# The first round's tile list made in two parts behind the last softmax, and the last batch's gate, choice and ranks woven with the first dense tiles

## The chip, the cores and the metric

The kernel runs on one core of one Trainium2 chip. Its time is the device time of one execution in microseconds (us), and the number that counts is the median over runs. Inside a core five engines work beside one another, each through its own list of instructions in order: PE (TensorE, matrix products; its weight loads are shown apart as PEld), DVE (VectorE), ACT (ScalarE), POOL (GpSimd) and SP (SyncE, which here only issues DMAs and reads values into registers). An instruction waits for others through semaphores. DMAs issued by POOL and by SP go to two different queues that share sixteen DMA engines.

## The reference: what is computed

Attention over chunks, and then a mixture of experts on its result.

```python
for c in range(nc):                       # 24 chunks of 32 queries
    q_c = q[:, :, c*32:(c+1)*32]
    k_full = concat(mem_k, k[:, :, left:right])   # 8 memory keys + up to 56 keys around the chunk
    a = softmax(q_c @ k_full.T / 8)
    out[:, :, c*32:(c+1)*32] = a @ v_full
x = out as (3072 tokens, 512)             # 4 batches of 768 tokens, 8 heads of 64
y_dense = relu(x @ w1_dense) @ w2_dense
logits = x @ w_gate                       # 8 experts
expert = argmax(logits); gate_w = softmax(logits)[expert]
y_moe[t] = gate_w[t] * (relu(x[t] @ w1[expert[t]]) @ w2[expert[t]])
return y_dense + y_moe
```

All matrices of the experts are 512 by 512.

## The kernel before

Sixteen attention steps come first, one for each pair of heads of each of the four batches (`for i in range(NPAIR)`, step 15 is the last). A step computes its own values and, ahead of time, the scores and the softmax of the next step. Its parts: `scores` (PE), `maximum` and `softmax` (DVE, then an exponential on ACT), `copy_v(i, 0)` on POOL and `copy_v(i, 1)` on DVE (line 333, they copy rows of the values that two chunks share, and wait for those rows' DMA), `probs_back` (PE transposes, ACT copy), `values` (PE, line 418), `scaled` (DVE, lines 429 and 430, giving x of the pair), `gate_part` (six PE transposes of x, line 450, copied by ACT, line 453), `gate_sum` (PE, line 475, three products with the gate's weights) and `gate_add` (DVE, lines 486 and 488, which adds that into the batch's logits).

When the four pairs of a batch are done, its tokens are routed: `logits` (two PE transposes, line 494), `choose` (DVE, lines 505 to 519, and an exponential on ACT, line 521), `ranks` (PE, lines 529 to 536: how many earlier tokens took the same expert), `rank` (DVE, lines 546 to 556: the token's row, `row_i`), and `rows_out`: six indirect DMAs from POOL (line 566) that write the token records to a buffer in DRAM, `x_reg`, sorted by expert. For batches 0 to 2 this happens inside later attention steps, for batch 3 behind the last step.

From the sorted buffer the tokens come back in tiles of 128 rows, all of one expert: `fetch(s)` on SP (line 172), `transposed(s)` (four PE transposes, line 186, three DVE operations, lines 189 to 191), `dense_first` and `dense_second` (PE, lines 200 and 215, with ACT's `h` and `yd`, lines 205 and 218). Which tiles there are stands in a list. `list_a` (lines 603 to 632, on DVE, with one PE product for the counts, line 593) lists the NA = 11 tiles that the first three batches fill whole: their first rows go to `src_i`, their experts to `et_i`, and `lim` tells `list_b` where it goes on. `bases(lo, hi)` loads rows of `src_i` into SP's registers (line 162), and only then can SP issue these fetches. `list_b` (a generator in two parts) does the same for the remaining 16 to 20 tiles, once batch 3 has its rows. Six buffers hold fetched tiles, so fetch 6 waits until tile 0 has been read.

The order on each engine is written out by hand: it is the order of the calls. POOL's queue carries in this region the row writes of batch 2, `copy_v(15, 0)`, eight weight loads (line 115), the row writes of batch 3 and eight more weight loads. PSUM banks for transposes and counts come from `bank()`, two in turn. Behind the 27 dense tiles come 27 expert tiles (`experts`), each of which stages its first-layer weights on DVE (line 878), does two layers on PE (lines 200 and 891), adds on DVE (line 896) and writes its rows with an indirect DMA from POOL (line 900).

Of the kernel before, what the change touches and what calls it, by code (L numbers as in the profile page):

```python
# [20 lines left out]
def kernel(  # L21
# [14 lines left out]
    nc = tc.nc  # L36
# [123 lines left out]
    def bases(lo, hi):  # L160

        _, vals = nc.values_load_multi_w_load_instructions(
            src_i[0:1, lo:hi], engines=(SP_,),
            min_val=0, max_val=E * ROWS - 128,
            skip_runtime_bounds_check_because="a tile ends at an expert's last row",
        )
        for i, val in enumerate(vals):
            base_of[lo + i] = val
# [39 lines left out]
    def dense_first(s):  # L208
        first_layer(s, w1d_sb)
# [117 lines left out]
    def copy_v(pi, hh):  # L327

        vt = vw[pi % NV]
        p0 = hh * KEYS  # L330
        n = CTX - CHUNK
        eng = nc.vector if hh else nc.gpsimd
        eng.tensor_copy(  # L333
            vt[p0 + CHUNK:p0 + CTX, :NCH - 1, hh, :D], vt[p0:p0 + n, 1:, hh, :D]
        )
# [206 lines left out]
    def rank(b):  # L542

        oh, rec, rk_ps = bat[b]["oh"], bat[b]["rec"], bat[b].pop("rk")
        val = r_work.tile([128, T, E], F32, tag="val", name="val")
        nc.vector.tensor_tensor(val, rk_ps, oh, ALU.mult)
        here = r_work.tile([128, E, 1], F32, tag="here", name="here")
        nc.vector.reduce_sum(here, oh.rearrange("p t e -> p e t"), axis=AX.X)
        sm = r_work.tile([128, T, 1], F32, tag="sm", name="sm")
        nc.vector.reduce_sum(sm, bat[b]["pr"], axis=AX.X)  # L550
        nc.vector.reciprocal(rec[:, :, GC:GC + 1], sm)
        rk = r_work.tile([128, T], F32, tag="rk", name="rk")
        nc.vector.reduce_sum(rk, val, axis=AX.X)
        row_i = b_work.tile([128, T], I32, tag="row_i", name="row_i")
        nc.vector.tensor_copy(row_i, rk)
        nc.vector.tensor_tensor(seen_bf, seen_bf, here[:, :, 0], ALU.add)
        bat[b]["row"] = row_i
# [45 lines left out]
    def list_a():  # L603
        cnt = ends()
        ni = r_work.tile([128, E], I32, tag="ni", name="ni")
        nc.vector.tensor_copy(ni, cnt)
        nc.vector.tensor_scalar(ni, ni, 7, None, ALU.logical_shift_right)
        nf = r_work.tile([128, E], F32, tag="nf", name="nf")
        nc.vector.tensor_tensor(nf, ni, reg25, ALU.subtract)
        cumulate(nf, cumA[:, 1:, None])  # L610
        nc.vector.tensor_scalar(cumA[:, 1:], cumA[:, 1:], float(NA), None, ALU.min)
        dA = r_work.tile([128, E], F32, tag="dA", name="dA")
        nc.vector.tensor_tensor(dA, cumA[:, 1:], cumA[:, :E], ALU.subtract)
        jump = r_work.tile([128, E], F32, tag="jump", name="jump")
        nc.vector.tensor_scalar(jump, dA, -128.0, float(ROWS), ALU.mult, ALU.add)
        ind = r_work.tile([128, NA, E], F32, tag="ge", name="ind")
        nc.vector.tensor_tensor(
            ind, slot_no[:, :NA, None].to_broadcast([128, NA, E]),
            cumA[:, None, 1:].to_broadcast([128, NA, E]), ALU.is_ge,
        )  # L620
        ef = r_work.tile([128, NA], F32, tag="ef", name="ef")
        nc.vector.reduce_sum(ef, ind, axis=AX.X)
        nc.vector.tensor_copy(et_i[:, :NA], ef)
        nc.vector.tensor_tensor(
            ind, ind, jump[:, None, :].to_broadcast([128, NA, E]), ALU.mult
        )
        bs = r_work.tile([128, NA], F32, tag="bs", name="bs")
        nc.vector.reduce_sum(bs, ind, axis=AX.X)
        nc.vector.tensor_tensor(src_i[:, :NA], bs, base_a, ALU.add)
        nc.vector.scalar_tensor_tensor(  # L630
            lim, dA, 128.0, reg0, op0=ALU.mult, op1=ALU.add
        )
# [116 lines left out]
    for i in range(NPAIR):  # L749
        b, hp = divmod(i, NP)  # L750
        routing = hp == 1 and b > 0
        if routing:
            gate_add(i - 2)
        if i + 4 < NPAIR:
            load_qk(i + 4, "q")
        if i + 3 < NPAIR:
            load_v(i + 3)
        if i == NPAIR - 1:
            bases(0, NA)
            for s in range(6):  # L760
                fetch(s)
        if i + 1 < NPAIR:
            copy_v(i + 1, 0)
            scores(i + 1)
        if i + 4 < NPAIR:
            load_qk(i + 4, "k")
        if i < 2:
            clear_side(i + 2, nc.gpsimd)
        if routing:
            logits(b - 1)  # L770
        if i:
            scaled(i - 1)
        if routing:
            choose(b - 1)
        if i:
            probs_back(i)
            gate_part(i - 1)
        if routing:
            ranks(b - 1)
        if i + 1 < NPAIR:  # L780
            maximum(i + 1)
            if routing:
                rank(b - 1)
            softmax(i + 1)
            copy_v(i + 1, 1)
        values(i, range(TB))
        if i + 2 < NPAIR:
            transpose_qk(i + 2)
        values(i, range(TB, T))
        if i > 1 and not routing:  # L790
            gate_add(i - 2)
        if i == NPAIR - 2:
            list_a()
        if i:
            record(i - 1)
            gate_sum(i - 1)
        for _ in range(w_steps.get(i, 0)):
            load_w(*w_todo.pop(0), parts=2)
        if routing:
            rows_out(b - 1, range(T if b == B - 1 else T // 2))  # L800
        if hp == 2 and 0 < b < B - 1:
            rows_out(b - 1, range(T // 2, T))
        if i == 1:
            (ones, upper, upto, slot_no, slot128, desc, pcol, tok, base_a, reg25,
             reg0) = constants()
        if i == 7:
            fill_out()

    last_p = NPAIR - 1
    scaled(last_p)  # L810
    transposed(0)
    gate_add(last_p - 1)
    transposed(1)
    gate_part(last_p)
    dense_first(0)
    for _ in range(4):
        load_w(*w_todo.pop(0))
    fetch(6)
    gate_sum(last_p)
    transposed(2)  # L820
    record(last_p)
    gate_add(last_p)
    dense_first(1)
    logits(B - 1)
    choose(B - 1)
    dense_second(0)
    fetch(7)
    dense_first(2)
    ranks(B - 1)
    rank(B - 1)  # L830
    rows_out(B - 1)
    dense_second(1)
    transposed(3)
    dense_first(3)
    dense_second(2)
    transposed(4)
    parts = list_b()
    next(parts)
    for s in range(4, NA):
        if s + 4 < NA:  # L840
            fetch(s + 4)
        if s + 1 < NA:
            transposed(s + 1)
        dense_first(s)
        dense_second(s - 1)
        if s == 5:
            for _ in parts:
                pass
# [137 lines left out]
```

## Time and profile before

| what | us |
|---|---|
| median of 3 runs | 256.66 (256.04 to 257.15) |
| the profiled execution | 255.87 |
| its span, first to last instruction | 254.2 |
| PE busy, of the span | 203.7 (80%) |
| DVE busy | 163.5 (64%) |
| POOL busy | 138.2 (54%) |
| ACT busy | 129.7 (51%) |

The profile is of one execution; its rows are in microseconds from the start of the span. A row of the timeline gives the start, the busy time, the engine, the line of the kernel, the operation, what it writes and reads, and in brackets how long the engine had been idle before and who ended that. A row of the chain that ended last gives the start, the length and the link. A row by line or tile gives the shortest, median and longest duration in ns and the first and last start.

### The profile page before, as it was taken

The page shows a single profiled execution, that of the slowest core. Times are in us where ns is not written, and L with a number is a line of the kernel's source. Part 1 is how long each engine was busy: PE and PEld are TensorE (multiplying, and loading weights), DVE is VectorE, ACT ScalarE, POOL GpSimd, SP SyncE. Part 2 cuts the span into 40 slices and gives each one's busy share as a digit, 9 for nine tenths or more (in the row PEclk, how much of TensorE's full clock was granted, in tenths as well). Part 3 has the DMA queues.
Part 4 walks back from the last instruction along what each step waited for, and adds up shares of the span by engine and source line. Part 5 has one row for each costly group of instructions (what it writes and reads, how often), then busy time and mean ns, then how long its engine had stood idle before and what let it go on. Part 6 is the DMA issues. An engine that isn't in the chain of part 4 may idle for free.

```text
span 254.2 us, 8004 instructions
## 1 busy us (share of the span) xinstructions
PE 203.7 (80%) x3147; PEld 149.9 (59%) x3147; DVE 163.5 (64%) x390; ACT 129.7 (51%) x201; POOL 138.2 (54%) x197
## 2 busy tenths in 40 slices
PE   1576778887877788877478899799998999999960
PEld 1464556665655666656246577577776676666640
DVE  5757998889997998768823482222233677777740
ACT  6353757738766677756123546356565332323210
POOL 8929982509891589938910387000000476766760
PEclk9999979999999999997767999999999999999997
DMA  5998999995999799999699949999900133322231
GB/s 88 189 163 134 153 146 145 156 127 132 205 155 262 142 156 173 195 197 228 94 195 243 206 129 121 241 232 228 182 0 3 61 148 124 154 113 118 93 129 70
DMA packets 60424, 38.33 MB, mean 151 GB/s; under 512 B 36190, under 2 KB 58078, under 8 KB 60384
## 3 DMA queue, kind: packets, MB, share of 16 engines
q0 software_dynamic: 21616, 25.20, 51.7%
q1 hardware_dynamic: 38768, 12.58, 25.1%
q8 instruction: 27, 0.44, 0.8%
q14 instruction: 13, 0.11, 0.2%
HBM read 42.97 MB, written 11.30 MB: 214 GB/s over the span
## 4 chain that ended last, share of the span: by engine, by line
issue 28%; DMA 21%; POOL 16%; PE 13%; DVE 13%; SPq 4%; ACT 2%; POOLq 1%; DVEq 0%; ACTq 0%
POOL out_dram L900 13%; DMA vw<-in_v_dram 11%; DMA wgate<-in_moe_w_gate_dram 3%; DMA w_all<-in_moe_w_dram 3%; DVE vw L333 3%; DMA xg<-x_reg 3%; DVE kbd L358 3%; POOL x_reg L566 2%; PE at_ps L475 2%; PE av L418 2%; PE tp L450 2%; PE tp L345 2%; PE at_ps L408 2%; SPq L303 1%; DMA mk_sb<-in_mem_k_dram 1%
## 5 line engine op out<-in xcount | busy, mean ns | idle before, releaser
L900 POOL DMA_INDIRECT out_dram<-y,dst_i x27 | 31.9, 1183 | 57.0 <-DVE y L896 56.8
L205 ACT ACTIVATE h<-sc 128x512 bf16<-128x512 f32 x54 | 32.2, 597 | 53.3 <-PE sc L200 53.3
L566 POOL DMA_INDIRECT x_reg<-rec,row_i x24 | 24.6, 1024 | 39.9 <-issue 24.1
L418 PE MATMUL av<-vw,at 128*32 128x130 f32 x768 | 33.9, 309 | 3.7 <-issue 2.3
L200 PEld LDWEIGHTS <-w_st 128*128 128x128 bf16 x432 | 26.0, 97 | 9.5 <-issue 3.4
L333 POOL COPY vw<-vw 24x1472 f32<-24x1472 f32 x16 | 24.1, 1506 | 11.2 <-DMA vw<-in_v_dram 10.8
L418 PEld LDWEIGHTS av<-vw,at 128*32 128x32 f32 x768 | 24.3, 122 | 9.3 <-issue 6.7
L200 PEld LDWEIGHTS <-w1d 128*128 128x128 bf16 x432 | 26.2, 100 | 1.6 <-DVE xT_A L189 0.7
L333 DVE COPY vw<-vw 24x1472 f32<-24x1472 f32 x16 | 21.2, 1322 | 5.7 <-DMA vw<-in_v_dram 5.4
L189 DVE COPY xT_B<-tp 128x512 bf16<-128x512 bf16 x16 | 6.8, 424 | 24.8 <-PE tp L186 24.8
L410 ACT COPY at<-at_ps 128x768 f32<-128x768 f32 x16 | 12.8, 799 | 19.5 <-PE at_ps L408 19.3
L878 DVE COPY w_st<-w_all 128x2048 bf16 x27 | 18.4, 685 | 3.8 <-PE sc L200 2.7
L450 PE MATMUL tp<-identity_f,x 128*128 128x128 f32 x96 | 15.8, 306 | 5.9 <-DVE x L430 5.3
L453 ACT COPY xT<-tp 128x384 f32<-128x384 f32 x32 | 14.2, 488 | 12.0 <-PE tp L450 11.8
L402 ACT ACTIVATE a<-dif 128x768 f32<-128x768 f32 x16 | 13.7, 855 | 11.7 <-DVE dif L397 9.2
L215 PE MATMUL av<-w2d,h 128*128 128x512 bf16 x72 | 18.5, 379 | 0.0
L891 PE MATMUL av<-w_all,h 128*128 x72 | 18.4, 378 | 0.0
L391 DVE TENSOR_REDUCE mx<-sc 128x12 f32<-128x768 f32 x16 | 15.3, 954 | 3.7 <-PE sc L381 3.6
L200 PE MATMUL sc<-xT_B,w_st 128*128 128x128 bf16 x256 | 16.9, 219 | 0.7 <-issue 0.7
L358 DVE COPY kbd<-tp 64x768 bf16<-64x768 bf16 x16 | 15.2, 949 | 3.2 <-PE tp L345 2.8
L200 PE MATMUL sc<-xT_B,w1d 128*128 128x128 bf16 x256 | 16.9, 219 | 0.0
L450 PEld LDWEIGHTS tp<-identity_f,x 128*128 128x128 f32 x96 | 12.0, 155 | 7.6 <-issue 5.9
(151 smaller groups left out, 402.1 us busy)
## 6 DMA issues: line engine op xcount, KB each, us to landing
w_all<-in_moe_w_dram POOLq DMA_DIRECT2D x12, 512.0 KB, 15.2
xg<-x_reg SPq DMA_DIRECT2D x27, 129.0 KB
q_bf<-in_q_dram POOLq DMA_DIRECT2D x16, 192.0 KB, 6.3
k_bf<-in_k_dram POOLq DMA_DIRECT2D x16, 192.0 KB, 6.3
vw<-in_v_dram SPq DMA_DIRECT2D x32, 96.0 KB
vw<-in_v_dram SPq DMA_DIRECT2D x32, 88.0 KB
w_all<-in_moe_w_dram POOLq DMA_DIRECT2D x8, 256.0 KB, 8.7
vw<-in_mem_v_dram SPq DMA_DIRECT2D x32, 48.0 KB
```

The source lines that it names most:

```text
L200: nc.tensor.matmul(ph[:, f, :], w[:, d, f * 128:(f + 1) * 128], xT[:, d, :], start=(d == 0), stop=(d == DT - 1),)
L205: nc.scalar.activation(h_sb, ph, AF.Relu)
L215: nc.tensor.matmul(pd, h_d[:, f, :], w2d_sb[:, f, :], start=(f == 0), stop=(f == FT - 1))
L333: eng.tensor_copy(vt[p0 + CHUNK:p0 + CTX, :NCH - 1, hh, :D], vt[p0:p0 + n, 1:, hh, :D])
L358: lo = nc.vector.tensor_copy(dst[:D, 0], srcv[:D])
L391: nc.vector.reduce_max(mx, scv, axis=AX.X)
L418: nc.tensor.matmul(av[cc * CHUNK:(cc + 1) * CHUNK, t // TB, (t % TB) * W2:(t % TB + 1) * W2], at[:, t, cc * CHUNK:(cc + 1) * CHUNK], vt[:, ...
L450: nc.tensor.transpose(xtt[:, t * 128:(t + 1) * 128], xb[:, t0 + t, :], identity_f32)
L566: inst = nc.gpsimd.indirect_dma_start(x_reg, bass.IndirectOffsetOnAxis(ap=row_i[:, t:t + 1], axis=0), rec[:, t, :], None,)
L878: nc.vector.tensor_copy(w_st[:, None], w1_all[:, bass.ds(e_dve.pop(s), 1), :, :])
L891: nc.tensor.matmul(py, h_e[:, f, :], w2_all[:, bass.ds(e, 1), f, :], start=(f == 0), stop=(f == FT - 1),)
L900: inst = nc.gpsimd.indirect_dma_start(out, bass.IndirectOffsetOnAxis(ap=dst_i[:, s:s + 1], axis=0), y, None, bounds_check=N_tokens - 1, oo ...
```

## The change

The first list is made earlier and is a generator with a `yield` now. In step 14 its first part stands right behind `softmax(15)`, together with `gate_add(12)`, ahead of `copy_v(15, 1)` on DVE and ahead of `values(14)` on PE; it goes as far as `src_i`. The second part (`et_i` and `lim`) is run behind the third dense tile's first layer. The registers for the eleven bases are loaded in two goes, six and five, with the first six fetches between them. In `rank`, three sums that do not need the ranks stand ahead of the product that does. Behind the last attention step the order of the calls is another: both first tiles are transposed ahead of `gate_add(14)`; tile 2's transposes come ahead of the gate's sum; tile 0's second layer, and no longer tile 1's first layer, comes between the gate's sum and the logits; tile 1's first layer and tile 3's transposes come between choice and ranks; fetches 8 to 10 are asked for earlier in the order of calls; tile 3 is done in the loop.

```diff
@@ rank(b)
-        val = r_work.tile([128, T, E], F32, tag="val", name="val")
-        nc.vector.tensor_tensor(val, rk_ps, oh, ALU.mult)
         here = r_work.tile([128, E, 1], F32, tag="here", name="here")
         nc.vector.reduce_sum(here, oh.rearrange("p t e -> p e t"), axis=AX.X)
         sm = r_work.tile([128, T, 1], F32, tag="sm", name="sm")
         nc.vector.reduce_sum(sm, bat[b]["pr"], axis=AX.X)
         nc.vector.reciprocal(rec[:, :, GC:GC + 1], sm)
+        val = r_work.tile([128, T, E], F32, tag="val", name="val")
+        nc.vector.tensor_tensor(val, rk_ps, oh, ALU.mult)
@@ list_a()
-        ind = r_work.tile([128, NA, E], F32, tag="ge", name="ind")
+        ind = r_work.tile([128, NA, E], F32, tag="ind", name="ind")
...
+        skip = r_work.tile([128, NA, E], F32, tag="ge", name="skip")
+        nc.vector.tensor_tensor(
+            skip, ind, jump[:, None, :].to_broadcast([128, NA, E]), ALU.mult
+        )
+        bs = r_work.tile([128, NA], F32, tag="bs", name="bs")
+        nc.vector.reduce_sum(bs, skip, axis=AX.X)
+        nc.vector.tensor_tensor(src_i[:, :NA], bs, base_a, ALU.add)
+        yield
         ef = r_work.tile([128, NA], F32, tag="ef", name="ef")
         nc.vector.reduce_sum(ef, ind, axis=AX.X)
         nc.vector.tensor_copy(et_i[:, :NA], ef)
-        nc.vector.tensor_tensor(
-            ind, ind, jump[:, None, :].to_broadcast([128, NA, E]), ALU.mult
-        )
-        bs = r_work.tile([128, NA], F32, tag="bs", name="bs")
-        nc.vector.reduce_sum(bs, ind, axis=AX.X)
-        nc.vector.tensor_tensor(src_i[:, :NA], bs, base_a, ALU.add)
@@ the attention steps
         if i == NPAIR - 1:
-            bases(0, NA)
+            bases(0, 6)
             for s in range(6):
                 fetch(s)
+            bases(6, NA)
...
             softmax(i + 1)
+            if i == NPAIR - 2:
+                gate_add(i - 2)
+                parts = list_a()
+                next(parts)
             copy_v(i + 1, 1)
...
-        if i > 1 and not routing:
+        if i > 1 and not routing and i != NPAIR - 2:
             gate_add(i - 2)
-        if i == NPAIR - 2:
-            list_a()
@@ behind the last step
     scaled(last_p)
     transposed(0)
+    transposed(1)
     gate_add(last_p - 1)
-    transposed(1)
     gate_part(last_p)
     dense_first(0)
     for _ in range(4):
         load_w(*w_todo.pop(0))
     fetch(6)
+    transposed(2)
     gate_sum(last_p)
-    transposed(2)
+    gate_add(last_p)
     record(last_p)
-    gate_add(last_p)
-    dense_first(1)
+    dense_second(0)
     logits(B - 1)
     choose(B - 1)
-    dense_second(0)
+    dense_first(1)
     fetch(7)
-    dense_first(2)
+    transposed(3)
     ranks(B - 1)
     rank(B - 1)
     rows_out(B - 1)
     dense_second(1)
-    transposed(3)
-    dense_first(3)
-    dense_second(2)
+    dense_first(2)
+    for _ in parts:
+        pass
+    fetch(8)
     transposed(4)
     parts = list_b()
     next(parts)
-    for s in range(4, NA):
-        if s + 4 < NA:
-            fetch(s + 4)
-        if s + 1 < NA:
+    for s in range(3, NA):
+        if 4 <= s and s + 5 < NA:
+            fetch(s + 5)
+        if 5 <= s + 1 < NA:
             transposed(s + 1)
         dense_first(s)
         dense_second(s - 1)
```

## The prediction

> **What bounds the kernel now.** I read the page first, then the windows by stage, then the chain that ended last, and then engine by engine the timeline between 117 and 162 us, where all edits lie.
>
> ```profile
> span 254.2 us, 8004 instructions
> ```
>
> ```profile
> 131.00:134.00 3.00, 0.76 (x11) 0.26 (x6) 1.70 (x5) 0.00 (x0) 0.00 (x0) 0.99 1.17 240
> 134.00:138.00 4.00, 3.90 (x32) 2.94 (x32) 0.67 (x4) 1.43 (x3) 0.00 (x0) 0.57 1.19 243
> 138.00:161.00 23.00, 20.97 (x252) 15.29 (x246) 10.69 (x58) 12.86 (x23) 12.48 (x20) 1.00 0.89 167
> 161.00:192.00 31.00, 30.30 (x367) 23.02 (x368) 9.14 (x49) 17.17 (x29) 0.00 (x0) 1.00 0.84 165
> 192.00:254.00 62.00, 52.16 (x564) 36.04 (x561) 36.60 (x54) 18.48 (x31) 33.89 (x53) 0.97 0.26 104
> ```
>
> The columns of the windows are the stretch, its length, and the busy time of PE, PEld, DVE, ACT and POOL, then the granted clock, the DMA share and GB/s. From 161 us on PE has no holes (30.30 of 31.00), and the expert stage behind it runs at PE's and POOL's pace. No edit touches that part, so what the change is worth is the shift of the point at 161 us. That point hangs on two chains: the list of the first round's tiles, up to PE's first dense tile at 132.80; and from there gate, choice, ranks, six row writes and the fetch of tile 11. Ahead of 132.80 PE is nearly idle (0.76 of 3.00): that is where time can be won.
>
> ```profile
> 117.93 0.96 DVE L397 TENSOR_TENSOR dif<-sc,mx 128x768 f32<-128x768 f32 x1
> 119.93 0.96 DVE L333 COPY vw<-vw 24x1472 f32<-24x1472 f32 x1 [1.04 <-DMA vw<-in_v_dram]
> 120.92 0.42 DVE L486 COPY lgT<-at_ps 96x256 f32<-96x256 f32 x1
> 121.26 0.15 DVE L606 CAST ni<-tp 128x8 int32<-128x8 f32 x1
> 121.45 0.67 DVE L607 TENSOR_SCALAR ni<-ni 128x8 int32<-128x8 int32 x1
> 122.87 0.17 DVE L611 TENSOR_SCALAR cumA<-cumA 128x8 f32<-128x8 f32 x1
> 123.63 0.24 DVE L622 TENSOR_REDUCE ef<-ind 128x11 f32<-128x88 f32 x1
> 123.99 0.30 DVE L624 TENSOR_TENSOR ind<-ind,jump 128x88 f32<-128x88 f32 x1
> 124.63 0.17 DVE L629 TENSOR_TENSOR src_i<-bs,base_a 128x11 int32<-128x11 f32 x1
> 125.25 0.96 DVE L430 TENSOR_TENSOR x<-av,rs 128x768 f32<-128x768 f32 x1
> ```
>
> ```profile
> 120.06 2.03 POOL L333 COPY vw<-vw 24x1472 f32<-24x1472 f32 x1
> 122.05 5.96 POOL L115 DMA_DIRECT2D w_all<-in_moe_w_dram  x8
> ```
>
> ```profile
> L162 SPq TENSOR_LOAD <-src_i x3: 1270/1408/2296, 124.8 to 167.5; - x3
> L333 POOL COPY vw<-vw x16: 1404/1409/2037, 11.3 to 120.1; 24x1472 f32<-24x1472 f32 x16
> L640 DVE TENSOR_SCALAR ni<-ni x1: 171/171/171, 146.4 to 146.4; 128x8 int32<-128x8 int32 x1
> ```
>
> The first chain, in the chain that ended last and on PE:
>
> ```profile
> 103.30 10.51 DMA vw<-in_v_dram
> ...
> 126.52 0.38 SPq L172
> ...
> 127.09 6.83 DMA xg<-x_reg
> ```
>
> ```profile
> 132.80 0.40 PE L186 MATMUL tp<-identity,xg 128*128 128x128 bf16 x4 [1.47 <-DMA xg<-x_reg]
> 133.97 0.40 PE L186 MATMUL tp<-identity,xg 128*128 128x128 bf16 x4 [0.77 <-DMA xg<-x_reg]
> 134.20 1.58 PE L450 MATMUL tp<-identity_f,x 128*128 128x128 f32 x6
> 135.58 1.91 PE L200 MATMUL sc<-xT_A,w1d 128*128 128x128 bf16 x16
> 137.43 0.84 PE L475 MATMUL at_ps<-xT,wgate 128*32 128x256 f32 x6
> 139.66 0.35 PE L494 MATMUL tp<-identity_f,lgT 96*128 96x96 f32 x2 [0.17 <-DVE lgT L488]
> 139.85 1.03 PE L215 MATMUL av<-w2d,h 128*128 128x512 bf16 x4
> 140.72 1.06 PE L200 MATMUL sc<-xT_A,w1d 128*128 128x128 bf16 x16
> 161.02 0.40 PE L186 MATMUL tp<-identity,xg 128*128 128x128 bf16 x4 [0.85 <-DMA xg<-x_reg]
> ```
>
> The reader sees: src_i is written at 124.80, SP's load of it into registers takes 1.41, the first fetch goes out at 126.52, and its tile is on PE at 132.80: 6.28 after the issue. The gate's transposes (L450) follow the second tile, and end at 135.78.
>
> **Part 1: the list, earlier and in two parts.** Before, gate_add and the list stand behind `copy_v(15,1)` (L333), for which DVE waits 1.04 on a DMA, and behind PE's values. After, they start where the softmax's `dif` ends, at 118.89. gate_add takes 0.34 to the next start (120.92 to 121.26), so the list's cast starts near 119.26. The matmul that counts now stands ahead of `values(14)` on PE; it waits for a bank that ACT's copy of the gate's transposes frees, and what it delays, `values(14)`, is needed only by `scaled(14)`, which DVE reaches later than the list's end; so it hides, and if that cover is gone it costs that bank's wait and one small matmul.
>
> The list does not keep its own pace. L607 took 0.67 where the same operation in the second list (L640) took 0.17, and it ended at 122.12, just behind POOL's copy (120.06 plus 2.03 is 122.09). So such an operation stands still while POOL copies. In the new order L607 runs before POOL's copy begins (POOL is held by its last row write until 120.06, unchanged), but L611, another scalar operation, falls into it. Without DVE's copy beside it POOL's takes 1.41, so to about 121.47; L611 ends just after. From L611's start to the end of src_i was 122.87 to 124.80, 1.93; without ef and its cast (123.63 to 123.99, 0.36, now behind) 1.57. Counted from 121.45 that is **src_i at 123.0, 1.8 earlier**. The ends: 121.9 if nothing waits (119.26 plus the 3.54 from L606 to src_i, less 0.36 for ef and the 0.50 by which L607 was too long), 123.55 if the operation before L611 waits as well, since it and the sum behind it (0.26 each) are then late too. I take 123.0, by L607's row.
>
> The load of six values instead of eleven: its rows give 1.27 to 2.30 for ten or eleven, so the count does not set it; I keep 1.41. First fetch at 124.7, 1.8 earlier. The second load, of five values, stands behind the sixth fetch on SP; behind it waits only fetch 6, which waits for tile 0's buffer anyway, so it costs nothing; without that cover it would cost tile 6 its 1.3 to 2.3, six tiles behind the first on PE. ef and its cast (0.36) and lim move behind `rank`, in front of nothing but tile 4's copies.
>
> Moved behind src_i is `copy_v(15,1)`, 0.96: `scaled(14)` starts at about 124.4 (L430 stood at 125.25), so x of the last pair comes 0.85 earlier, near 131.1; what waits for it on PE is only the gate's transposes.
>
> When does the fetch land? It meets POOL's eight weight loads (issued from 122.05, now from about 121.5). Issue to use was 6.28 at 126.52, some 4.5 behind the first weight load, and at tile 11 it was 7.66, 2.1 behind the first load of the next series:
>
> ```profile
> 153.36 0.33 SPq L172 DMA_DIRECT2D xg<-x_reg  x1
> ```
>
> Now it is 3.2 behind, so between them: 6.7. **Tile 0 at 131.4, tile 1 at 132.6, the gate's transposes end at 134.4: 1.4 earlier.** The ends are 3.6, the rows' own median to landing, and 10.51, the row at 103.30.
>
> ```profile
> x_reg<-rec,row_i POOLq DMA_INDIRECT x8, 3.6
> ```
>
> **Part 2: gate, choice and ranks woven.** Counted from the first layer's start (135.58): before, the logits' transposes come 4.08 later. After: first layer 1.85, tile 2's transposes 0.4, gate sum 0.77, second layer of tile 0 0.87, together 3.9; its h is there, since ACT has the 1.2 of the transposes and the sum for one activation. Choice starts 0.2 earlier. After choice DVE waited for PE's ranks, and now does tile 3's copies in that hole (0.42 and two small ones, 0.55 in all by my estimate), and three sums of `rank` that need no ranks stand ahead of `val`:
>
> ```profile
> 143.07 0.42 DVE L189 COPY xT_A<-tp 128x512 bf16<-128x512 bf16 x1
> ```
>
> ```profile
> 150.28 0.97 POOL L566 DMA_INDIRECT x_reg<-rec,row_i  x1 [0.22 <-issue]
> ```
>
> ```profile
> DVE val L546 <- PE tp L536: 0.8, 1, 0.8
> ...
> PE sc L200 <- DVE xT_A L189: 0.5, 1, 0.5
> PE tp L186 <- DVE xT_A L189: 0.5, 1, 0.5
> ```
>
> That wait of 0.8 shrinks to the copies' 0.55 and a little: another 0.2. **row_i, and with it the six row writes, come 0.4 earlier** relative to the gate. PE's own two waits of 0.5 (for tile 3's and 4's copies) go too, but that only lets PE end its dense work sooner and stand longer than the 0.85 ahead of 161.02: tile 11 is what is late next. Its fetch went 3.1 behind the last row write's start (150.28), held by the second list's load of 2.30. The second list now moves about 0.9 earlier relative to the gate (PE's two waits), the rows 0.4, so the rows hold it. The weight loads behind the rows on POOL shift with them; fetch 8 is issued a tile earlier, when tile 2's buffer is free. All these are hidden by the same work as before.
>
> **Sum.** 1.35 (tiles) and 0.4 (weaving): 1.75 us. The profiled execution took 255.87 us, 1.7 outside its span, so it would be 254.1. The three runs' median is 256.66, 0.8 above it; taken from the median: **254.9 us**. About 0.5% (1.28 us) is what a measurement can tell from no change.
>
> The clock may add or take: at 134 to 138 us it was 0.57, so that the first dense layer took 1.91 against 1.06 later. If the slow stretch ends a window earlier, 0.85 are won; if it keeps its place, tile 0's second layer falls into it and costs as much. I take neither and keep both for the range.
>
> **The rivals.**
> A, the fetch no longer meets a backlog, and x is late next. If the latency is under 5.2, tile 1 is there before x (131.1); then DVE's copies of two tiles (0.42 each and their small ones) behind x set the gate's transposes, which end near 133.0, 2.8 earlier: 3.2 in all, 253.5 us. For it: fewer weight loads are queued 3.2 into the series. Against: 7.66 at 2.1 into it. The Trainium skill, DMA: Bandwidth & Descriptors, section Queues, rings and completion order, says that each DMA engine goes round its queues packet by packet, so that a fetch on another queue should not wait for a backlog; by that the time is A's. The trace speaks against it: 6.28 and 7.66 us.
>
> B, the list hardly gains. If the operation before L611 waits for POOL's copy too (src_i 123.55) and the load takes 2.30, the fetch goes at 126.16, only 0.36 earlier; with the weaving 0.8, 255.9 us: no change that can be told. The Trainium skill, SBUF — State Buffer, section Who interferes with whom, speaks for the first half: by it an instruction of VectorE with two inputs in SBUF also waits for a GpSimd instruction that reads SBUF, as scalar operations do. The trace agrees for the scalar kind (L607, 0.67); no row here shows it for two inputs.
>
> C, slower: the earlier fetch falls into the thick of the weight series and takes as long as the load at 103.30, 10.51. Tile 0 would be at 135.2, 2.4 later than now; less 0.4 that is 258.7 us. From a latency of 8.5 the change loses, from 9.8 by more than 0.5%. For it: latency rose from 6.28 to 7.66 as the fetch came nearer to the series' start. Against: 10.51 was a load of many small pieces.
>
> **How the numbers follow.** The forecast 0.50, A 0.17, B 0.23, C 0.10. The forecast's own range, from its bounds of src_i and the clock, is 254.0 to 256.0; some of it (0.10) lies above 255.38, the 0.5% mark. Faster: 0.17 and 0.40, 0.57. Within 0.5%: B and that 0.10, 0.33. Slower 0.10. The range of 8 in 10 leaves out most of C and the far half of A: 253.2 to 256.9.
>
> **What would show it.** Right: src_i's write (L627 now) near 123.0, the first fetch at 124.7, tile 0's transposes at 131 to 131.6, the gate's transposes ending near 134.4, the last row write 1.75 earlier, at 148.5, tile 11 near 159.3, PE without holes after it. Step one is wrong if L611 or L598 shows more than 1.2 us, or L162's load more than 1.5; the third if the first fetch's use is more than 7 us behind its issue; the weaving if DVE still waits for L536 or PE for h. The whole is wrong if tile 11 comes no earlier though the rows do, or if holes appear behind it, such as experts waiting for weights.

## The result, and the profile after

The changed kernel takes 253.41 us (median of 6 runs, 250.94 to 255.82), beside 256.66 before (6 runs of the same chip now, 253.81 to 258.64): a ratio of 0.988, 95% interval 0.9835 to 0.9928. The forecast was 254.9. The profiled execution took 253.07 us. In two later sets of runs the same kernel came to 0.994 (0.990 to 0.998) and 0.979 (0.972 to 0.987). The gain is real, since all three intervals lie below 1; at 0.6 to 2% it is about as large as forecast (0.7%) or larger, and its size is known no better than that. (Ratios are taken over each kernel's fast executions alone, those within 1.5% of its fastest, so that 0.979 rests on two of six runs and the 0.981 of `hold_w2` below on three of seven; the quotients of the medians are 0.987, 0.993 and 0.991 for the change and 0.991 for `hold_w2`.)

The windows of the changed kernel, cut as before at tile 11 and at the experts (columns as there):

```profile
span 251.3 us, 8000 instructions
```

```profile
131.00:134.00 3.00, 1.49 (x32) 0.84 (x25) 1.74 (x5) 0.00 (x0) 0.00 (x0) 1.00 1.18 244
134.00:138.00 4.00, 3.82 (x43) 2.62 (x42) 1.85 (x8) 2.27 (x4) 0.00 (x0) 1.00 1.19 243
138.00:158.00 20.00, 19.39 (x239) 14.53 (x238) 10.29 (x57) 11.40 (x20) 12.47 (x20) 1.00 1.01 195
158.00:189.00 31.00, 30.18 (x366) 22.88 (x366) 9.03 (x49) 17.75 (x30) 0.00 (x0) 1.00 0.87 170
189.00:251.00 62.00, 52.36 (x565) 36.12 (x563) 36.63 (x54) 18.48 (x31) 33.55 (x53) 0.97 0.26 104
```

Tile 11 is on PE at 158 and no longer at 161; the stages behind it are what they were (30.18 of 31.00 against 30.30, and 52.36 of 62.00 against 52.16). So the whole gain lies ahead of tile 11, as the prediction had it. Two things are new: the granted clock from 134 to 138 is 1.00 where it was 0.57, and the stretch up to tile 11 is denser (19.39 of 20.00).

The list on DVE, POOL beside it, the loads of bases by line, and the two issues that frame the second chain:

```profile
120.56 0.96 DVE L397 TENSOR_TENSOR dif<-sc,mx 128x768 f32<-128x768 f32 x1
121.95 1.33 DVE L607 TENSOR_SCALAR ni<-ni 128x8 int32<-128x8 int32 x1
124.03 0.17 DVE L611 TENSOR_SCALAR cumA<-cumA 128x8 f32<-128x8 f32 x1
125.35 0.17 DVE L627 TENSOR_TENSOR src_i<-bs,base_a 128x11 int32<-128x11 f32 x1
```

```profile
121.84 1.41 POOL L333 COPY vw<-vw 24x1472 f32<-24x1472 f32 x1 [0.47 <-DMA vw<-in_v_dram]
...
148.20 0.97 POOL L566 DMA_INDIRECT x_reg<-rec,row_i  x1 [0.22 <-issue]
```

```profile
L162 SPq TENSOR_LOAD <-src_i x4: 946/1174/2295, 125.6 to 164.6; - x4
```

```profile
126.78 7.52 SPq L172 DMA_DIRECT2D xg<-x_reg  x7
...
151.36 0.33 SPq L172 DMA_DIRECT2D xg<-x_reg  x1
```

PE, from the first tile to the first tiles of the second round:

```profile
132.85 0.40 PE L186 MATMUL tp<-identity,xg 128*128 128x128 bf16 x4 [0.88 <-DMA xg<-x_reg]
133.88 0.40 PE L186 MATMUL tp<-identity,xg 128*128 128x128 bf16 x4 [0.63 <-DMA xg<-x_reg]
...
134.80 0.55 PE L450 MATMUL tp<-identity_f,x 128*128 128x128 f32 x3 [0.18 <-DVE xT_A L189]
135.18 1.06 PE L200 MATMUL sc<-xT_A,w1d 128*128 128x128 bf16 x16
```

```profile
157.98 0.40 PE L186 MATMUL tp<-identity,xg 128*128 128x128 bf16 x4
159.20 0.40 PE L186 MATMUL tp<-identity,xg 128*128 128x128 bf16 x4 [0.82 <-DMA xg<-x_reg]
```

In this execution the last softmax ended at 121.52, 2.63 later than in the profile before. Nothing that the edit moves stands ahead of it; the same operation of earlier steps was already 1.1 later at 40 us and 1.0 later at 102 us; the cause is not known. So the steps have to be counted from the softmax's end:

| us behind the end of `dif` | before | forecast | after | won | forecast |
|---|---|---|---|---|---|
| src_i written | 5.91 | 4.11 | 4.00 | 1.91 | 1.8 |
| first fetch issued | 7.63 | 5.81 | 5.26 | 2.37 | 1.8 |
| tile 0 on PE | 13.91 | 12.51 | 11.33 | 2.58 | 1.4 |
| gate's transposes end | 16.89 | 15.51 | 13.83 | 3.06 | 1.4 |
| last row write starts | 31.39 | 29.6 | 26.68 | 4.71 | 1.75 |
| tile 11 on PE | 42.13 | 40.4 | 36.46 | 5.67 | 1.75 |

5.67 less the later start of 2.63, and 0.16 that the end of the span came later behind tile 11, is the 2.9 by which the spans differ.

### The profile page after: what moved, and what is told of

Its sections match the earlier page's. It is cut to its first block, busy times and chain, and to the rows that moved or that the text cites. A ratio compares the mean times of both kernels' runs of the same rounds, so it can differ in the third digit from the quotient of the medians.

```text
span 251.3 us, 8000 instructions
## 1 busy us (share of the span) xinstructions
PE 200.5 (80%) x3147; PEld 148.5 (59%) x3147; DVE 164.5 (65%) x390; ACT 129.4 (51%) x201; POOL 137.9 (55%) x197
## 4 chain that ended last, share of the span: by engine, by line
DMA 37%; issue 25%; POOL 14%; DVE 10%; PE 7%; SPq 3%; POOLq 1%; ACT 0%; DVEq 0%
DMA vw<-in_v_dram 24%; POOL out_dram L906 13%; DMA vw<-in_mem_v_dram 5%; DMA xg<-x_reg 4%; DMA w_all<-in_moe_w_dram 3%; DVE vw L333 2%; DVE kbd L358 2%; PE at_ps L475 1%; POOL x_reg L566 1%; SPq L303 1%; PE at_ps L408 1%; POOL scratch L560 1%; PE av L418 1%; PE av L215 1%; PE tp L450 1%
## 5 line engine op out<-in xcount | busy, mean ns | idle before, releaser
L418 PE MATMUL av<-vw,at 128*32 128x130 f32 x768 | 30.9, 291 | 2.4 <-issue 2.0
L200 PEld LDWEIGHTS <-w_st 128*128 128x128 bf16 x432 | 26.0, 97 | 9.5 <-issue 3.1
L333 POOL COPY vw<-vw 24x1472 f32<-24x1472 f32 x16 | 23.4, 1462 | 13.3 <-DMA vw<-in_v_dram 8.5
L418 PEld LDWEIGHTS av<-vw,at 128*32 128x32 f32 x768 | 22.5, 115 | 7.6 <-issue 5.5
L200 PEld LDWEIGHTS <-w1d 128*128 128x128 bf16 x432 | 25.5, 98 | 1.4 <-issue 0.9
L450 PE MATMUL tp<-identity_f,x 128*128 128x128 f32 x96 | 15.2, 297 | 5.6 <-DVE x L430 5.0
L475 PE MATMUL at_ps<-xT,wgate 128*32 128x256 f32 x96 | 10.5, 400 | 9.0 <-DVE lgT L488 5.8
L200 PE MATMUL sc<-xT_B,w_st 128*128 128x128 bf16 x256 | 16.9, 219 | 0.6 <-issue 0.4
L408 PE MATMUL at_ps<-identity_f,a 128*128 128x128 f32 x96 | 15.8, 308 | 1.6 <-ACT a L402 1.6
L200 PE MATMUL sc<-xT_B,w1d 128*128 128x128 bf16 x256 | 16.9, 219 | 0.0
## 6 DMA issues: line engine op xcount, KB each, us to landing
w_all<-in_moe_w_dram POOLq DMA_DIRECT2D x8, 256.0 KB, 10.7
```

The source lines that it names most:

```text
L200: nc.tensor.matmul(ph[:, f, :], w[:, d, f * 128:(f + 1) * 128], xT[:, d, :], start=(d == 0), stop=(d == DT - 1),)
L333: eng.tensor_copy(vt[p0 + CHUNK:p0 + CTX, :NCH - 1, hh, :D], vt[p0:p0 + n, 1:, hh, :D])
L408: nc.tensor.transpose(at_ps[:, t, :], a_sb[:, t, :], identity_f32)
L418: nc.tensor.matmul(av[cc * CHUNK:(cc + 1) * CHUNK, t // TB, (t % TB) * W2:(t % TB + 1) * W2], at[:, t, cc * CHUNK:(cc + 1) * CHUNK], vt[:, ...
L450: nc.tensor.transpose(xtt[:, t * 128:(t + 1) * 128], xb[:, t0 + t, :], identity_f32)
```

## The experiments

The experiments ran on three chips, each with its own runs of the kernel before: 271.60 us (35 runs) in the first set, 256.19 (11) in the second, 269.40 (29) in the third. Only ratios carry from one to another. Every kernel was also profiled once; the distances below are from the rows of those timelines (tile 0, first layer: PE's rows of L186 and L200; gate to row_i: from the end of L450 to the end of L555; load: the first row of the load of bases).

| kernel | dif to src_i | load | fetch to tile 0 | dif to tile 0 | first dense layer | gate to row_i | ratio (95%) |
|---|---|---|---|---|---|---|---|
| before | 5.91 | 1.41 | 6.28 | 13.91 | 1.91 | 7.17 | 1 |
| after | 4.00 | 0.95 | 6.07 | 11.33 | 1.06 | 5.54 | 0.988 (0.984, 0.993) |
| changed_again | 3.32 | 0.94 | 5.88 | 10.45 | 1.91 | 7.44 | 0.994 (0.990, 0.998) |
| list_early | 3.33 | 0.94 | 5.79 | 10.38 | 1.06 | 6.14 | 0.988 (0.983, 0.992) |
| woven | 5.27 | 1.38 | 5.47 | 12.44 | 1.91 | 7.00 | 1.003 (0.998, 1.008) |
| copy_on_act | 3.43 | 0.94 | 5.41 | 10.09 | 1.60 | 6.04 | 0.989 (0.984, 0.995) |
| changed_2 | 3.50 | 0.94 | 3.87 | 10.21 | 1.92 | 6.50 | 0.979 (0.972, 0.987) |
| list_2 | 4.28 | 0.94 | 6.13 | 11.67 | 1.91 | 7.18 | 0.982 (0.977, 0.986) |
| list_warm | 4.27 | 0.94 | 4.69 | 10.21 | 1.06 | 6.14 | 0.987 (0.983, 0.991) |
| change_warm | 4.30 | 0.94 | 6.19 | 11.74 | 1.91 | 6.80 | 0.986 (0.981, 0.992) |
| list_whole | 3.90 | 1.38 | 5.83 | 11.41 | 1.06 | 5.54 | 0.999 (0.994, 1.003) |
| early_w1 | 2.92 | 0.94 | 5.68 | 9.85 | 1.89 | 6.32 | 0.994 (0.987, 1.001) |
| hold_w2 | 3.42 | 0.95 | 5.83 | 10.50 | 1.56 | 6.00 | 0.981 (0.971, 0.991) |
| early_hold | 2.85 | 0.95 | 5.94 | 10.05 | 1.91 | 7.47 | 0.997 (0.992, 1.001) |

**The two parts apart.** `changed_again` is the change unedited. `list_early` takes only the list; the ending and `rank` stay as before:

```diff
     ...
+    for _ in parts:
+        pass
     parts = list_b()
     next(parts)
```

> The whole change once more, as the measure for the parts. Theory P (the path: list 1.4 us, weaving 0.4 us, what the result shows above that is chance of the executions): ratio to before about 0.993, and in the profile src_i about 4.0 us behind the end of the last softmax's difference (before 5.9). Theory C (the clock: PE's denser work ahead of the first dense layer ends the slow stretch earlier, 0.9 to 2 us on top): ratio about 0.988 again, and the first dense layer takes 1.06 us, not 1.91. Theory D (tile 11's fetch meets less traffic, 1.0 us): use of tile 11 again about 6.6 us behind its issue, not 7.7.

> The list in two parts behind the last softmax and the bases in two goes alone; the end in the order of before. P: 1.4 us off, ratio about 0.9945; first fetch about 5.3 us behind the end of the softmax's difference (before 7.6). C: nearly the whole of what the change brings, ratio 0.988 to 0.991, with the first dense layer at 1.06 us. If the fetch only waits longer for its data: ratio 0.997 to 1.0.

`woven` takes only the other half: `rank` and the ending of the change, with `list_a()`, `bases(0, NA)` and `gate_add` where they were.

> The new order behind the last step and in rank alone; the list as before. P: 0.4 us off, ratio about 0.9985, not to be told from no change; row_i ends about 5.5 us behind the gate's transposes' end (before 7.2), of which the clock's state takes or gives up to 1. C: ratio about 0.9985 too, since nothing ahead of the first dense layer is denser. D: if weaving is what spares tile 11's fetch, ratio 0.995.

Medians: 269.81 (12 runs), 268.18 (12) and 272.27, beside 271.60. The list alone shows at least the gain of the whole change, the weaving alone nothing that can be told: its interval reaches from 0.2% faster to 0.8% slower. But on this chip PE never stands waiting for a tile of the second round (none of PE's waits from 150 us on is for `xg`), so that rows written earlier had nothing to shorten at the end. On the chip of the second set PE does wait for such tiles in three of four profiles (1.6 to 1.9 us in all), and there `woven` was not run. The rows of DVE and PE say why the list helps, first with before's list (`woven`), then with the early one (`list_early`):

```profile
131.49 0.96 DVE L397 TENSOR_TENSOR dif<-sc,mx 128x768 f32<-128x768 f32 x1
...
137.55 0.17 DVE L629 TENSOR_TENSOR src_i<-bs,base_a 128x11 int32<-128x11 f32 x1
```

```profile
144.88 0.61 PE L186 MATMUL tp<-identity,xg 128*128 128x128 bf16 x4 [2.87 <-DMA xg<-x_reg]
```

```profile
130.54 0.96 DVE L397 TENSOR_TENSOR dif<-sc,mx 128x768 f32<-128x768 f32 x1
131.93 0.17 DVE L607 TENSOR_SCALAR ni<-ni 128x8 int32<-128x8 int32 x1
132.86 0.46 DVE L611 TENSOR_SCALAR cumA<-cumA 128x8 f32<-128x8 f32 x1
134.66 0.17 DVE L627 TENSOR_TENSOR src_i<-bs,base_a 128x11 int32<-128x11 f32 x1
```

```profile
141.87 0.40 PE L186 MATMUL tp<-identity,xg 128*128 128x128 bf16 x4 [1.91 <-DMA xg<-x_reg]
```

From the end of `dif` to tile 0 it is 12.43 in the first and 10.37 in the second by these rows, 2.06 less, and PE stands waiting for the tile in both.

**POOL's copy.** In the profile after, L607 stands for 1.33 while POOL copies (121.84 to 123.25) and goes on 0.03 behind it. `copy_on_act` gives that copy to ACT:

```diff
-            copy_v(i + 1, 0)
+            if i != NPAIR - 2:
+                copy_v(i + 1, 0)
...
                 next(parts)
+                copy_v(i + 1, 0, nc.scalar)
```

> The whole change, with POOL's copy of shared value rows of step 15 given to ACT, behind the softmax's exponential, so that DVE's list runs beside no POOL copy. If POOL's copy holds the list up (in the changed kernel the shift L607 took 1.33 us, 0.17 without a copy): L607 takes 0.17, src_i comes 1.0 to 1.2 us earlier, and as far as the fetch passes this on the ratio is 0.003 to 0.004 lower than the whole change's. If something else stretches L607: it stays above 0.6 us and the ratio is that of the change.

Median 269.42, ratio 0.989: between the change and the list alone, no gain that can be told. On this chip there was little to win, since POOL's copy did not meet L607 even in `list_early` (0.17) and `changed_again` (src_i 3.32 behind `dif`, 3.43 with ACT's copy). In the first result's profile and on the chip of the second set it meets a scalar operation of the list in four of five profiles (L607, in `list_warm` the one of `jump`, for 1.08 to 1.33 where it takes 0.17 to 0.33 alone), and src_i comes 4.00 to 4.30 behind the softmax, against 3.50 in the fifth. So the copy costs 0.5 to 0.8 of the list where it falls, and where it falls changes from chip to chip.

`copy_on_act` does not leave the list alone with DVE either, since POOL issues weight loads beside it. In five profiles of the two slower chips with these loads there the shift L611 takes 0.44 to 0.55; in `early_w1` and `early_hold` (below), where POOL issued none in that moment, it takes 0.17, and src_i comes 2.92 and 2.85 behind `dif`. So the issuing of loads seems to cost the list about 0.5 on these chips; no run isolates it.

**The order against the clock.** The list alone looked better than the whole change, and its profile had the fast clock in the first dense layer (1.06), the other one the slow clock (1.91). So both were run again, and both with matmuls of no use to keep PE busy:

```diff
+    def keep_warm(n):
+        for _ in range(n):
+            nc.tensor.matmul(sc[:, 0, :], identity, w1d_sb[:, 0, :], start=True, stop=True)
...
             probs_back(i)
+            if i == NPAIR - 1:
+                keep_warm(8)
...
     last_p = NPAIR - 1
+    keep_warm(4)
```

> The changed kernel, unedited, on another chip beside the list alone. If the first measurement (ratio 0.988) is the change's own, it comes to 0.985 to 0.992 of before; if the second one (0.994) is, to 0.990 to 0.998.

> The list alone (the two-part list behind the last softmax, the ending and the ranks in before's order), again. Theory W (the new ending order costs about 1 us by itself): 0.3 to 0.7% below the changed kernel, as in the first run. Theory C (the order is worth nothing, the two differ by the granted clock they happened to get): within 0.3% of the changed kernel, ratio to before about 0.99, and the profile with the longer time is the one with the cold first dense layer (1.91 us against 1.06).

> The list alone, and 12 matmuls of no use (identity times the dense weights, 512 wide) into the idle score bank: 8 before the transposes of x of pair 14 in the last step, 4 before the last pair's result is scaled. Theory C: the granted clock stays at 1.0 from about 124 to 137, the first dense layer takes 1.06 us, and the time falls by 0.9 to 1.7 us against the list alone where that one was cold; nothing (within 0.4 us) where it was warm. If the filler itself is in the way of the transposes, x of pair 14 gets to the gate later and the time rises by up to 1.5 us.

> The changed kernel with the same 12 matmuls. Theory C: equal to the list with the same matmuls within 0.3%, since both now have the warm clock. Theory W: 0.3 to 0.7% above it. The path as the prediction has it (rows written 0.4 us earlier by the order): 0.15% below it.

Medians: 253.87, 252.50, 253.29 and 253.89 (6 runs each), beside 256.19. The 0.979 of `changed_2` lies below both bands that were written down for it (by the medians it is 0.991, inside both). By their ratios change and list alone agree here (0.979 and 0.982, intervals overlapping); by the medians the list alone is below the change in all three pairs, by 0.6%, 0.5% and 0.2%. So whether the new order costs something, as theory W has it, stays open; that it wins something at the end is not shown. The useless matmuls win nothing in either kernel, so theory C's gain did not come. They did not even secure the clock: `list_warm` had the fast clock in the first dense layer, `change_warm` not.

Windows that are cut where the clock changes tell why. It stays full or half for stretches of 3.41 us or multiples of it. Here are the stretch ahead of the one in which the first dense layer starts, and that one itself, in before, after, `change_warm` and `list_warm`:

```profile
131.07:134.48 3.41, 1.17 (x14) 0.72 (x11) 1.82 (x6) 0.00 (x0) 0.00 (x0) 1.00 1.18 242
134.48:137.89 3.41, 3.31 (x28) 2.48 (x25) 0.48 (x3) 1.31 (x3) 0.00 (x0) 0.50 1.19 241
```

```profile
130.74:134.15 3.41, 1.90 (x43) 1.25 (x36) 1.74 (x5) 0.00 (x0) 0.00 (x0) 1.00 1.18 241
134.15:137.56 3.41, 3.23 (x38) 2.17 (x36) 1.85 (x8) 2.24 (x4) 0.00 (x0) 1.00 1.19 245
```

```profile
130.36:133.77 3.41, 1.20 (x12) 0.80 (x13) 1.10 (x7) 0.16 (x1) 0.00 (x0) 1.00 1.18 244
133.77:137.18 3.41, 3.41 (x29) 2.79 (x29) 0.77 (x5) 1.67 (x4) 0.00 (x0) 0.50 1.19 243
```

```profile
128.25:131.66 3.41, 2.90 (x61) 2.00 (x62) 1.50 (x3) 1.33 (x3) 2.32 (x5) 1.00 1.14 209
131.66:135.07 3.41, 2.53 (x32) 1.91 (x32) 1.12 (x7) 1.28 (x3) 0.00 (x0) 1.00 1.19 242
```

Behind 1.17 and 1.20 us of busy PE the clock is half, behind 1.90 and 2.90 it is full. It is so in all 14 profiles: where the first layer was slow, PE had been busy for 0.93 to 1.50 of the 3.41 us ahead of the slow stretch; where it was fast, for 1.78 to 3.15. So this clock goes with how much of the stretch PE spends standing for tile 0, and with where the 3.41 us happen to begin. That is the mechanism of theory C; its gain in time was not seen. The useless matmuls of `change_warm` ended at 130.36, just ahead of the stretch that counted, so they did not put theory C to the test.

A change that shortens PE's stand may therefore raise the clock as well. Over all runs the mean granted clock is 0.944 in `changed_again` against 0.927 before, and 0.961 in `changed_2` against 0.952; it is above before's in all twelve kernels run beside before. How much of the gain comes through the clock, and how much through the earlier tile itself, no run separates: `list_warm` has the highest mean clock of its set (0.970) and not the lowest time.

The table gives the local price of weaving and clock. With the fast clock, gate to row_i is 6.14 in before's order (`list_early`, `list_warm`) and 5.54 in the new one (after, `list_whole`); the end of the gate's transposes (after's stands above) and the write of row_i in `list_early` and in after:

```profile
143.91 0.55 PE L450 MATMUL tp<-identity_f,x 128*128 128x128 f32 x3 [0.18 <-DVE xT_A L189]
150.43 0.17 DVE L555 CAST row_i<-rk 128x6 int32<-128x6 f32 x1
```

```profile
140.71 0.17 DVE L555 CAST row_i<-rk 128x6 int32<-128x6 f32 x1
```

The weaving wins 0.60 there. With one slow stretch of 3.41 us, before's order takes 7.17 and 7.18 (before, `list_2`) and the new one 6.32 to 6.80 (`early_w1`, `changed_2`, `change_warm`), so it wins 0.4 to 0.9; the clock is worth 1.03 in this piece. In `woven`, `changed_again` and `early_hold` the slow stretch is twice as long, and the new order takes 7.00 to 7.47; before's order has no profile like that. The first layer met the slow clock in 8 of 14 profiles at full length (1.9) and in two by part, change and list alike.

**One list, early, but whole.** `list_whole` is the change with before's `list_a` called at the new place and its bases loaded in one go:

```diff
-            bases(0, 6)
+            bases(0, NA)
             for s in range(6):
                 fetch(s)
-            bases(6, NA)
...
-                parts = list_a()
-                next(parts)
+                list_a()
```

> The changed kernel with the list of the first round in one part at the new place (ef and et_i ahead of the bases again) and its bases loaded in one go of 11. If the early place is the gain: src_i about 0.4 us later behind the last softmax than in the change (two small reductions more), the load 1.38 to 1.41 us where the change has 0.94, so the first fetch 0.9 us later. Theory P (the fetch's issue sets tile 0): tile 0 and the end 0.9 us later, about 0.35%. Theory Q (weight loads that are queued ahead set tile 0, whenever its fetch is issued): tile 0 and the end as in the change, within 0.2%, the fetch's latency 0.9 us shorter (5.2 where the change has 6.1).

Median 268.51 (12 runs, ratio 0.999). The load of eleven values takes 1.38 where that of six takes 0.94, and tile 0 is on PE 11.41 behind the softmax, where the change on the slower chips has 10.45 (`changed_again`) and 10.50 (`hold_w2`, which is the change up to tile 11): 0.9 later, as theory P says. The fetch did not get shorter for being issued later (5.83 against 5.88), so theory Q falls. Of the 2.0 by which the change brings tile 0 forward on the two slower chips (from 12.44, in `woven`, to 10.45), the early place gives 1.0 and the cut into two parts the other 1.0, by one profile each. At the end the interval of `list_whole` (0.994 to 1.003) holds no gain as well as the 0.4% that 1.0 us would be, so the early place alone is not shown to reach the end. The unedited change was not run on this chip.

**What the fetch waits for.** `early_w1` takes the two weight loads of step 14 away from in front of the first fetch, `hold_w2` holds the second layers' loads back until tile 11 has landed, `early_hold` does both:

```diff
-    w_steps = {11: 1, 12: 2, 13: 1, 14: 2}
+    w_steps = {11: 2, 12: 3, 13: 1}
```

```diff
     bases(NA, NA + 10)
-    while w_todo:
-        load_w(*w_todo.pop(0))
     for s in range(NA, NA + 5):
         fetch(s)
+    nc.gpsimd.tensor_copy(scratch2, xg_of[NA][0:1, 0:1])
+    while w_todo:
+        load_w(*w_todo.pop(0))
```

> The changed kernel with the two expert-weight loads of step 14 (2 times 512 KB, issued some 3 us ahead of the first fetch) moved to steps 11 and 12. Theory Q: the first fetch finds at most the ending's loads ahead; tile 0 is on PE 2.8 to 4.5 us behind its fetch's issue (5.4 to 6.3 in the runs of the change so far but one), so 1.5 to 3 us earlier; the gate's transposes then wait for x of the last pair instead, so at most 1.5 us of it reaches the end: ratio about 0.5% under the change's. Theory P (6.1 us is what a fetch takes whatever is queued): no difference in latency, and nothing at the end.

> The changed kernel with the eight second-layer expert loads (4 MB, issued from 149 on) held on GpSimd until the first tile of the second round has landed. Theory D (those loads ahead of the fetch make its 6.6 to 8 us): tile 11 is on PE 2.8 to 4.5 us behind its fetch's issue, PE's wait there stays away and the time falls by 0 to 1 us: the tile has slack where PE still has first-round tiles to do. If the loads are then late for the experts' second layers (from about 192 on), PE waits there and the time rises.

> Both: step 14's weight loads moved to steps 11 and 12, and the second-layer loads held behind tile 11. Theory Q with D: the sum of the two, ratio 0.5 to 0.9% under the change's. Theory P: as the change, within 0.2%.

Medians 268.22 (12 runs), 266.96 (7) and 268.34 (12), beside 269.40. `early_w1` missed what was expected of theory Q: the fetch took 5.68 as ever. POOL's timeline shows it, and the DMA queues between the fetch's issue (132.53) and the first packet of its tile (136.07):

```profile
125.13 1.41 POOL L333 COPY vw<-vw 24x1472 f32<-24x1472 f32 x1
126.50 0.80 POOL L115 DMA_DIRECT2D w_all<-in_moe_w_dram  x1
127.50 1.54 POOL L115 DMA_DIRECT2D w_all<-in_moe_w_dram  x2 [0.20 <-issue]
130.97 0.75 POOL L115 DMA_DIRECT2D w_all<-in_moe_w_dram  x1 [1.93 <-issue]
```

```profile
q0 software_dynamic: 722, 0.71, 122.3%
```

With step 14's loads gone, POOL comes to the ending's four loads earlier, and these (512 KB each) are the new backlog: 0.71 MB of weights pass ahead of the tile. In the change it is 0.54 MB, by the same view of its first fetch:

```profile
q0 software_dynamic: 557, 0.54, 106.3%
```

`hold_w2` shows the other end. Its tile 11 is asked for at 163.53 with no weights queued, and POOL, which waits for that tile, sees it at 165.62; the weights follow:

```profile
165.62 0.18 POOL L918 COPY scratch<-xg 1x1 f32<-1x1 f32 x1 [7.75 <-DMA xg<-x_reg]
166.32 6.04 POOL L115 DMA_DIRECT2D w_all<-in_moe_w_dram  x8 [0.52 <-DMA xg<-x_reg]
```

That is 2.1 from issue to use, where fetches behind weights took 5.4 to 6.3. But PE comes to tile 11 only at 171.27 in this kernel:

```profile
171.27 0.61 PE L187 MATMUL tp<-identity,xg 128*128 128x128 bf16 x8
```

The tile lay there for 5.6, so the wait behind the weights goes away as theory D has it, and there is nothing to gain by it here. This chip is one of those on which PE never stands waiting for a tile of the second round, with or without the hold; where PE does, the hold was not tried. The ratio of 0.981 is the lowest of its set, but `early_hold`, which holds the same loads, has 0.997. Whether holding them wins anything stays open; no version is shown to beat the change.

## Why the prediction was right, and where its steps were not

The forecast of 254.9 was 1.5 above the first result (253.41); its ratio of 0.993 lies in the interval of the second measurement (0.990 to 0.998), at the edge of that of the first and above that of the third. The first result is 0.2 above the lower end of the stated range (253.2 to 256.9) and below the forecast's own range (254.0 to 256.0): that it lies inside is owed to the room left for rival A, whose way it did not come, so there is luck in it. Its frame held: the end moved by what was won ahead of tile 11, and the win began at the list. The sum was too small, and its parts were shared out wrongly.

*The list, 1.8 earlier: right in size (1.91), wrong in its instruction.* The step said that L607 would run ahead of POOL's copy and L611 fall into it. In the profile after, L607 stood 1.33 and L611 took 0.17: POOL's copy started 0.32 behind the softmax's end, where the step had taken 1.17 from the profile before (120.06), and so it was there ahead of L607. An operation of that kind does stand still while POOL copies. The Trainium skill, SBUF — State Buffer, section Who interferes with whom, calls the shared port an exclusive lock for a whole instruction; the trace agrees: 0.17 alone, 1.33 beside a copy of 1.41.

*The load, kept at 1.41: mis-sized, and the plainest miss.* The step read rows of 1.27 to 2.30 for ten or eleven values as showing that the count does not matter. None had six. Six took 0.94 or 0.95 in eleven profiles, eleven 1.38 to 1.41 in three: 0.45 won, and in `list_whole` it is gone.

*The fetch, 6.7 for 6.28: wrong in direction.* It went down to 6.07. The step made latency a matter of how far into the weight series the fetch falls, from two rows. Over 14 profiles it was 5.4 to 6.3 where 1.5 to 3 MB of weights had been issued ahead of it, and less where little had been issued (3.87 with 0.5 MB or less, 4.69 with 0.75): shorter, not longer, close behind the series' start. So the 0.4 that the sum lost to a longer fetch was not lost.

*The weaving, 0.4: right locally, not seen at the end.* It wins 0.60 from gate to row_i by rows of the same clock. DVE's wait for the ranks went, and PE's waits of 0.5 for copies too. But one for h came, which the prediction had named as a sign against this step, as the waits of PE show:

```profile
PE tp L186 <- DMA xg<-x_reg: 2.3, 3, 0.9
PE sc L200 <- ACT h L205: 0.5, 1, 0.5
```

At the end `woven` alone is 1.003, at best 0.2% faster.

*The clock, taken at nothing with 0.85 for the range: the largest miss of the profiled pair.* It gave 1.03 from gate to row_i alone. The step took the slow stretch as something that keeps its place or ends a window earlier; the windows above show that it hangs on PE's busy time in the 3.41 us ahead, 1.17 before and 1.90 after. In the two later profiles of the same kernel (`changed_again`, `changed_2`) the first layer was slow again, so taking nothing fits those, and the first result was lucky in this term.

*Tile 11.* It was to be as late as its rows; 7.66 from issue to use became 6.62, and PE found it there (157.98 without a wait). The last row write to tile 11 so gave 0.96 where the sum had nothing.

Rival A's time (253.5) was closest to the result, by another way than its own: the backlog was there, and x was not late. The rule beside it was read too strongly: the Trainium skill, DMA: Bandwidth & Descriptors, section Queues, rings and completion order, lets an engine drain a whole packet, typically 9 to 17 and at most 64 descriptors, before it turns to another queue. The trace shows 0.54 to 0.73 MB let past, 35 to 46 pieces of 1 KB for each of 16 engines, more than the typical packet and less than the largest; whether they were one packet no view here shows. B's first half partly came true (the longest stand was 1.33, of the scalar operation; in that profile no operation with two inputs stood), but its load of 2.30 did not. C's 10.51 came nowhere: no first fetch of the 14 profiles took more than 6.28.

## What to carry to other kernels

For a list that opens a stage, put it right behind its last input, write out first what the next engine needs, and let that engine load only the first few values: here it took all of this together to show at the end. Before taking work out of the way of a transfer, ask what its engine will issue in its place: taking two loads from in front of the fetch only pulled the next four up. A piece of order that wins 0.6 us by its rows may still not be seen at the end; look first whether the engine still waits behind it. And PE's stand can cost twice: its own length, and half of the clock in the 3.41 us that follow.

## What the runs showed of the hardware that was not expected

A fetch on SP's queue waited for some of POOL's weights, not for all of them: in the twelve profiles with 1.5 MB or more issued ahead of it, its first packet moved 3.5 to 4.1 us behind the issue, after 0.54 to 0.73 MB of weights; with an empty queue (tile 11 in `hold_w2`) 1.0 behind it.

The clock of PE fell to half for stretches of 3.41 us or multiples. In the 14 profiles, from 20 us on, it fell 72 times, never behind a stretch in which PE had been busy for more than 1.85 of 3.41 us; and it stayed full 793 times, never behind less than 1.45. Over the 35 to 83 runs of each set, 1.5 to 1.9 us less time goes with each 0.01 of mean granted clock; which of the two brings the other, that does not say.

The kernel before takes 256 to 257 us in the first result and on the chip of the second set, and 269 to 272 on the two other chips. On those PE, ACT and DVE stand together for 3.0 to 4.5 us in the dense stage, in every kernel profiled there, as in `changed_again`:

```profile
PE sc L200 <- DVE dst_i L191: 3.8, 1, 3.8
```

No profile of the faster chips has that hole. Its cause was not found. All kernels of those sets have it, but it may bear on what they can show: the hole lies ahead of tile 11, and on those chips PE never waited for that tile, so work on the second chain (the weaving, the held weights) had nothing to win there.
